# A Fourier mixer and a sentence-level expert layer on one core: the start of the pipeline and its last tile rearranged

## The chip, the cores and the metric

The kernel runs on one core of a Trainium2 chip. The time is that of the device in microseconds; the median of three runs is taken. The engines are named as in the profile: PE (TensorE, matmuls), PEld (its weight loads), DVE (VectorE), ACT (ScalarE), POOL (GpSimd) and SP (SyncE). SP and ACT start transfers on instruction rings; POOL starts those of the software queue, which can also convert fp32 to fp16 on the way.

## The reference

The input x has 8 batches of 2496 rows by 256 columns. Each batch goes through a Fourier transform over its rows, a complex mix of the columns, a soft threshold and the inverse transform, and then through one of eight experts, chosen by the mean of its rows.

```python
X = np.fft.rfft(x, axis=1)
Yr = Xr @ w_r - Xi @ w_i + b_r
Yi = Xr @ w_i + Xi @ w_r + b_i
Y = sign(Y) * np.maximum(np.abs(Y) - 0.01, 0.0)      # real and imaginary part each
y = np.fft.irfft(Y, n=2496, axis=1)
# then, per batch:
logits = y.mean(axis=1) @ w_gate                      # e = argmax, g = its softmax probability
out = g * (np.maximum(y @ w1[e], 0.0) @ w2[e])        # 256 -> 1024 -> 256
```

## The kernel before

**Stages of a batch.** The 2496 rows are seen as 39 by 64. Matmuls with a table `wa` transform over the 39 (tile `pa`), then a mix with the weights `w4` (tile `pm`), a transform over the 64 with the tables `tf` and `tm` (tile `pb`; `tm` lives in a buffer of `V2`, so the profile prints it as V), then on DVE the bias and the threshold: z, its clip `cl`, and Y as their difference. The inverse starts with table `ti` (tile `pv`, cast to `V`), goes through a scratch in DRAM (`scr`), is read back as `V2`, and ends with table `wi` (tile `pi`, cast to `ysb`). The expert layer is `ph` (first product, relu to `hs`) and `po` (second product, scaled by the gate `gbc` into `ost` and stored).

Batches 0 and 1 take a short way (`add_attn_direct`): pa with x as the stationary operand, its cast to the buffer named `XB`, and for each of ten pairs of frequencies four matmuls of 512 columns into two `pm`, two casts to `Pt`, four matmuls into `pb`, then z, clip and Y. This needs only the two plain slots of `w4`, w_r and w_i. Batches 2 to 7 (`add_attn`) need also the slots 0 and 1, which hold w_i - w_r and -(w_r + w_i); `w_products` forms them on POOL.

**Order.** All instructions of a batch are put into a list of operations with costs and dependencies, and `Schedule.run` lays them out: again and again it takes the operation that can start first by its model, and emits it on its engine. Each engine then runs its instructions in this order; the model's times set the order alone. Copies out of PSUM may go to ACT or DVE. What is emitted before the list (the first loads, the dummies) has its arrival given as constants: `X0_AT` for the parts of input 0, `W_AT` for the weights, `T_AT` for the tables, `X1_AT` for input 1. Expert work of one batch is interleaved with the transforms of the next two.

**The start.** Input 0 has eleven chunks of columns in `xin0`. Chunks 0 to 3 come as fp32 into `xf` over the rings of SP and ACT in two halves and are cast on ACT and DVE; chunks 4 to 7 and 8 to 10 come over the software queue, converted on the way, into a view of `xin0` without gaps, so that several chunks of a row form one run. Then follow on POOL the weights as fp32 (`wr`, `wm`), the tables in three parts, the biases, and input 1. Nine dummy matmuls (`WARM`) on a zeroed tile `warm` stand ahead of the first pa. The casts of the weights (`w_cast`) are operations of the list.

**The end.** The last piece of the last batch (c == 4, sp == 1) fills a bank `po` with 2 times 256 columns from 16 matmuls, one copy takes both to `ost`, and two stores on SP bring out 128 and 64 rows. In the last batch these `po` rotate through two banks.

Of the kernel before, what the change touches and what calls it, by code (L numbers as in the profile page):

```python
# [10 lines left out]
FP16 = mybir.dt.float16  # L11
# [75 lines left out]

PEN = 0.2
SLACK = 2.5


class Op:
    def __init__(self, engs, occ, lat, emit, vt, deps, allocs, dma):
        self.engs, self.occ, self.lat, self.emit = engs, occ, lat, emit
        self.vt, self.deps, self.allocs, self.dma = vt, deps, allocs, dma
        self.done = self.after = None
        self.slack = SLACK


class Tok:  # L100
# [6 lines left out]
class Schedule:  # L107
# [52 lines left out]
        return t  # L160

    def run(self):
        free = dict.fromkeys(("PE", "ACT", "DVE", "SP", "POOL"), 4.0)
        free["POOL"] = 17.0
        ring = {"SP": 7.0, "POOL": 25.0}
        todo = sorted(self.ops, key=lambda o: o.vt)
        self.log = []
        while todo:
            best = None
            seen = {e: 0 for e in free}  # L170
            for o in todo:
                if all(seen[e] > 24 for e in o.engs):
                    continue
                r = self.ready(o)
                if r is None:
                    continue
                for e in o.engs:
                    seen[e] += 1
                    s = max(r, free[e])
                    if e == "DVE" and len(o.engs) > 1:  # L180
                        s += PEN
                    k = (s, o.vt, s + o.lat[e])
                    if best is None or k < best[0]:
                        best = (k, o, e)
            (s, _, _), o, e = best
            if e == "DVE" and len(o.engs) > 1:
                s -= PEN
            todo.remove(o)
            for k in o.allocs:
                self.hist.setdefault(k.tag, []).append(k)  # L190
            free[e] = s + o.occ[e]
            o.done = s + o.lat[e]
            if o.dma:
                other = "POOL" if e == "SP" else "SP"
                t = max(ring[e], s + 1.3)
                behind = max(0.0, ring[other] - t)
                if e == "SP":
                    ext = min(2.3 * o.dma, behind)
                    ring[other] += ext / 2.3
                else:  # L200
                    ext = min(0.43 * o.dma, behind)
                    ring[other] += min(2.3 * behind, o.dma)
                ring[e] = t + o.dma + ext
                o.done = ring[e] + o.slack
            self.log.append((s, e, o))
            o.emit(e)
# [3 lines left out]
def kernel(  # L210
# [27 lines left out]
        return ctx.enter_context(tc.tile_pool(name=name, bufs=bufs, **kw))  # L238

    XROW = 2 * D + 16  # L240
    WARM = 9
    BUFS = {"XT": 2, "hs": 2, "z": 3, "V": 6}
    cpool = pool("consts", 1)
    xpool = pool("xp", 2)
# [17 lines left out]
    def load_now(b, cuts, hold=None):  # L262
# [14 lines left out]

    xin0 = xpool.tile([117, NG // 2, XROW], FP16, name="xin").rearrange(  # L280
        "p g c -> p (g c)")[:, 0 : NG * D].rearrange("p (g c) -> p g c", c=2 * D)
    xf = hpool.tile([117, 4, 2 * D], FP32, name="hs")
    xv = x[0].rearrange("(a n) c -> a n c", n=N2)
    XH = ((0, 2), (2, 4))

    def x0_part(eng, j, c0, c1, dst):
        eng.dma_start(
            out=dst[39 * j : 39 * j + 39, c0:c1],
            in_=xv[:, 21 * j + 2 * c0 : 21 * j + 2 * c1, :].rearrange(
                "a (g i) c -> a g (i c)", i=2))  # L290

    warm = cpool.tile([P, 512], FP16, name="warm")
    nc.vector.memset(warm, 0.0)
    x0_part(nc.sync, 0, 0, 2, xf)
    x0_part(nc.scalar, 1, 0, 2, xf)
    x0_part(nc.sync, 2, 0, 2, xf)
    nc.scalar.dma_start(out=wa, in_=d_wa.ap())
    x0_part(nc.sync, 0, 2, 4, xf)
    x0_part(nc.scalar, 1, 2, 4, xf)
    x0_part(nc.sync, 2, 2, 4, xf)  # L300
    for c0, c1 in ((4, 8), (8, 11)):
        for j in range(3):
            x0_part(nc.gpsimd, j, c0, c1, xin0)
    wr = opool.tile([P, 2, D], FP32, name="ost")
    wm = opool.tile([P, 2, D], FP32, name="ost")
    nc.gpsimd.dma_start(out=wr, in_=w_r.rearrange("(t p) c -> p t c", p=P))
    nc.gpsimd.dma_start(out=wm, in_=w_i.rearrange("(t p) c -> p t c", p=P))

    pw = psum.tile([P, 512], FP32, tag="o", name="po", bufs=BANKS["o"])
    for _ in range(WARM):  # L310
        nc.tensor.matmul(pw, warm[:, 0:P], warm)
    tf = cpool.tile([P, NK1, P], FP16, name="tf")
    ti = cpool.tile([P, NK1, P], FP16, name="ti")

# [12 lines left out]
                                ap=[[0, P], [1, D]]))  # L327
        nc.gpsimd.dma_start(out=ti[:, k0:k9], in_=d_ti.ap()[:, k0:k9])
    bias2 = cpool.tile([P, D], FP32, name="bias2")


    w4 = cpool.tile([P, 2, 4, D], FP16, name="w4")
    e0 = cpool.tile([P, 1], FP16, name="e0")
    nc.sync.dma_start(out=e0, in_=d_e0.ap())
    wg = cpool.tile([P, 2, E], FP32, name="wg")
    nc.sync.dma_start(out=wg, in_=moe_w_gate.rearrange("(t p) e -> p t e", p=P))
    iot = cpool.tile([P, E], FP32, name="iot")
    nc.sync.dma_start(out=iot, in_=d_iota.ap())
    wi = cpool.tile([120, 117], FP16, name="wi")
    nc.sync.dma_start(out=wi, in_=d_wi.ap())  # L340
    wg16 = cpool.tile([P, 2, E], FP16, name="wg16")
    xin1 = load_now(1, (0, NG // 2))


    X0_AT, X1_AT = (4.3, 5.6, 8.8, 10.5), 25.0
    W_AT, T_AT = 11.2, (13.0, 15.5, 18.0)

# [2 lines left out]
    gbc_t, w1s_t, w2s_t = {}, {}, {}  # L352
    COPY = {"ACT": nc.scalar.copy, "DVE": nc.vector.tensor_copy}
    DIRECT = 2
    HOLD = 9
    LATE = -0.12
    PERIOD, SPAN, SHIFT = 49.5, 1.4, 0.6
# [1 line left out]
    def bank(nm, tag):  # L359
        return psum.tile([P, 512], FP32, tag=tag, name=nm, bufs=BANKS[tag])  # L360

    def w_cast(t, src):
        def emit(eng):
            COPY[eng](out=w4[:, :, t], in_=src)  # L364
        return S.evac(460, emit, 0, deps=[S.fixed(W_AT)])

    w_in = [w_cast(2, wr), w_cast(3, wm)]

    def bias_halves(eng):
        for i in range(2):  # L370
# [1 line left out]
            COPY[eng](out=bias2[s], in_=bias[s, i])  # L372
    b_in = S.evac(400, bias_halves, 0, deps=[S.fixed(T_AT[0])])

    def w_products(_):

        nc.gpsimd.tensor_sub(out=w4[:, :, 0], in0=wm, in1=wr)
        nc.gpsimd.tensor_scalar_mul(out=wr, in0=wr, scalar1=-1.0)
        nc.gpsimd.tensor_sub(out=w4[:, :, 1], in0=wr, in1=wm)
    w_late = S.op("POOL", 4.0, w_products, 1.0, deps=list(w_in))  # L380

    def wg_cast(eng):
        COPY[eng](out=wg16, in_=wg)
    wg_in = S.evac(20, wg_cast, 0.5, deps=[S.fixed(12.0)])
    t_in = [S.fixed(T_AT[0 if k1 < 4 else 1 if k1 < 12 else 2])
            for k1 in range(NK1)]
    first_V2 = S.tok("V2", 2)
# [2 lines left out]

    def x_cast(c):
        def emit(eng):
            COPY[eng](out=xin0[:, c], in_=xf[:, c])
        return S.evac(500, emit, -30 + c, deps=[S.fixed(X0_AT[c // 2])])

    x_cast_ops = [x_cast(c) for c in range(4)]
    c1, c2 = [S.fixed(X0_AT[2])], [S.fixed(X0_AT[3])]
    xdone = {0: [x_cast_ops[:2], x_cast_ops[2:], c1, c1, c2, c2],
             1: [S.fixed(X1_AT)]}
    xin_t[0], xin_t[1] = xin0, xin1  # L400
    xtok = {b: S.tok("xin", 2) for b in range(B)}
# [5 lines left out]
    def add_load(b):  # L407
        def emit(_):

            hold = V2_t[b - 2][0:1, 20, 0:2]  # L410
            xin_t[b] = load_now(b, (0, NG // 2), hold)
        vt = (b - 2) * PERIOD
        o = S.op("POOL", 1.6, emit, vt, deps=V2op[b - 2],
                 allocs=[xtok[b]],
                 dma=7.0)
        o.after = xdone[b - 1][0] if b > 2 else w_late
        xdone[b] = [o]

    def vt_of(b):
# [479 lines left out]
    def add_moe(b, y_ops, yk, gate):  # L899
        w, gb_op, wk = gate  # L900
        v0 = b * PERIOD
        for c, (ns, nl) in enumerate(NCH):
# [32 lines left out]
            for sp in range(2):  # L935
                tago = "o" if b < B - 1 else "h"
                ok = S.tok(tago, BANKS[tago])
                oc = {}
                for q in range(4):
                    v = v0 + PERIOD * (c * 8 + 6 + 4 * sp + q) / 44  # L940

                    def mm(_, sp=sp, q=q, nl=nl, cell=cell, oc=oc, tag=tago):
                        if q == 0:
                            oc["p"] = bank("po", tag).rearrange(
                                "p (i c) -> p i c", i=2)
                        i = q // 2
                        s0 = min((2 * sp + i) * P, nl - P)
                        for ft in range(4 * (q % 2), 4 * (q % 2) + 4):
                            nc.tensor.matmul(  # L949
                                oc["p"][:, i, :],  # L950
                                cell["hs"][:, ft, s0 : s0 + P],
                                w2s_t[b][:, ft, :],
                                start=(ft == 0), stop=(ft == E - 1))
                    m = S.mm([256] * 4, mm, v,
                             deps=h_ops[: 4 + 4 * (q % 2)],
                             after=m2 if q else None,
                             allocs=[ok] if q == 0 else [])
                    m2 = m
                    hk.rel.append(m)
                    wk.rel.append(m)  # L960

                def ev(eng, oc=oc):
# [4 lines left out]
                    else:  # L967
                        nc.vector.tensor_scalar_mul(out=ost, in0=oc["p"],
                                                    scalar1=gbc_t[b])
                e = S.evac(560, ev, v, deps=[m2, gb_op])  # L970
                ok.rel.append(e)

                def st(_, ns=ns, nl=nl, sp=sp, oc=oc):
                    ost = oc["o"]
# [6 lines left out]
                    else:  # L981
# [1 line left out]
                                          in_=ost[:, 0, :])  # L983
                        nc.sync.dma_start(out=out[b, r0 + P : ns + nl, :],
                                          in_=ost[64:P, 1, :])
                S.op("SP", 0.3, st, v, deps=[e], dma=0.75)

    for b in range(B):
        if b >= 2:
# [32 lines left out]
```

## Time and profile before

| what | value |
|---|---|
| median of 3 runs | 441.6 us (441.52 to 442.1) |
| span of the profiled run | 441.3 us |
| mean granted PE clock | 0.985 |
| PE busy | 424.7 us, 96% |
| DVE, ACT, POOL busy | 288.9, 328.6, 45.2 us |
| DMA | 80.31 MB, mean 182 GB/s |
| first pm, first z, first ph of batch 0 | start at 15.37, 19.58, 57.15 us |

A busy share is an average over the span. In the views in order of time the columns are start, duration, engine, line, operation and tiles, and in brackets the idle time of the engine before it with what ended it. In the chain of waits each piece has its start, its length and what it is, followed back from the last instruction. The table of stretches gives for each interval the busy time of the engines, the granted PE clock as a share of full speed, and what the DMA moved, counted as bytes written.

### The profile page before, as it was taken

The numbers are of one execution on the slowest core, as the hardware profiler recorded it, in microseconds if no ns is written. First come the engines' busy times: TensorE is split into PE (matmuls) and PEld (weight loads), VectorE is DVE, ScalarE is ACT, GpSimd is POOL, SyncE is SP. The second block draws the span as 40 slices with busy tenths as digits, with TensorE's granted clock in tenths as the row PEclk, the third lists the DMA queues.
The fourth block names the chain that finished last, engine by engine and source line by source line (L and its number), as shares of the span: only waits on it lengthen the run. The fifth ranks groups of instructions, "written<-read, shape, count | busy, mean of one in ns | idle before, by whom it ended". The sixth has DMA issues, their size and how long they took to land.

```text
span 441.3 us, 9023 instructions
## 1 busy us (share of the span) xinstructions
PE 424.7 (96%) x3387; PEld 300.9 (68%) x3387; DVE 288.9 (65%) x605; ACT 328.6 (74%) x636; POOL 45.2 (10%) x69
## 2 busy tenths in 40 slices
PE   4888999999999999999999999999999999999996
PEld 1555566677677866778677876778667787676764
DVE  1496965298866787687966887678976877322110
ACT  2787887777967778777867778677777778678674
POOL 5920300021000200020000200020000010000000
PEclk8698999999999999999999999999999999999999
DMA  7998996899979988699988999699978456472222
GB/s 166 276 183 176 170 211 162 239 207 206 202 230 213 186 174 220 199 199 215 189 256 193 177 189 220 219 199 197 188 211 230 127 134 126 130 161 67 71 73 91
DMA packets 98961, 80.31 MB, mean 182 GB/s; under 512 B 8000, under 2 KB 91889, under 8 KB 98917
## 3 DMA queue, kind: packets, MB, share of 16 engines
q1 hardware_dynamic: 75499, 58.17, 48.9%
q0 software_dynamic: 23184, 21.22, 30.3%
q8 instruction: 26, 0.43, 0.4%
q10 hardware_dynamic: 234, 0.35, 0.3%
q14 instruction: 18, 0.15, 0.1%
HBM read 59.36 MB, written 38.80 MB: 222 GB/s over the span
## 4 chain that ended last, share of the span: by engine, by line
PE 77%; DVE 9%; DMA 7%; ACT 3%; issue 2%; SPq 1%; POOL 0%; ACTq 0%; POOLq 0%; DVEq 0%
PE po L949 28%; PE ph L917 26%; PE pm L693 8%; PE pi L788 3%; PE pa L591 3%; PE pv L436 3%; DMA xin<-in_x_dram 3%; PE px L655 3%; PE pm L514 2%; DMA V<-scr 2%; DVE z L556 2%; DMA hs<-in_x_dram 2%; DVE Y L567 1%; DVE cl L565 1%; DVE Y L735 1%
## 5 line engine op out<-in xcount | busy, mean ns | idle before, releaser
L929 ACT ACTIVATE hs<-ph 128x512 f16<-128x512 f32 (+1 forms) x296 | 170.2, 592 | 73.6 <-PE ph L917 68.4
L949 PE MATMUL po<-w2s,hs 128*128 128x256 f16 x1280 | 180.6, 272 | 0.0
L917 PE MATMUL ph<-ysb,w1s 128*128 128x512 f16 (+1 forms) x640 | 179.8, 374 | 0.5 <-ACT ysb L809 0.5
L949 PEld LDWEIGHTS <-hs 128*128 128x128 f16 x1280 | 123.3, 98 | 51.7 <-issue 2.2
L917 PEld LDWEIGHTS <-w1s 128*128 128x128 f16 x640 | 61.4, 98 | 21.5 <-issue 0.7
L965 ACT ACTIVATE ost<-po,gbc 128x512 f32<-128x512 f32 x78 | 53.7, 689 | 13.0 <-PE po L949 13.0
L735 DVE TENSOR_TENSOR Y<-z,cl 64x512 f16<-64x512 f16 x120 | 50.4, 420 | 2.8
L707 DVE TENSOR_TENSOR tt<-pm,bias 128x512 f16<-128x512 f32 x60 | 38.6, 684 | 19.4 <-PE pm L693 19.4
L693 PE MATMUL pm<-w,XT 128*128 128x256 f16 x360 | 50.0, 273 | 0.4
L693 PEld LDWEIGHTS <-XT 128*128 128x128 f16 x360 | 34.2, 98 | 12.8 <-DVE XT L674 3.8
L931 DVE TENSOR_SCALAR hs<-ph 128x512 f16<-128x512 f32 (+1 forms) x24 | 16.5, 686 | 38.5 <-PE ph L917 33.8
L716 DVE TENSOR_TENSOR z<-pm,tt 128x512 f16<-128x512 f32 x60 | 38.4, 679 | 2.9 <-PE pm L693 2.9
L444 ACT CAST V<-pv 128x512 f16<-128x512 f32 x55 | 32.5, 612 | 2.1 <-PE pv L436 1.5
L803 DVE CAST ysb<-pi 128x468 f16<-128x468 f32 (+1 forms) x41 | 23.0, 582 | 16.8 <-PE pi L788 16.5
L663 DVE CAST XT<-px 128x512 f16<-128x512 f32 x32 | 21.6, 689 | 16.5 <-PE px L655 16.3
L601 ACT CAST A<-pa 120x512 f16<-120x512 f32 x50 | 28.1, 603 | 1.3 <-PE pa L591 1.1
L436 PE MATMUL pv<-Y,ti 128*128 128x256 f16 x160 | 25.9, 272 | 2.5 <-DVE Y L567 2.1
L803 ACT CAST ysb<-pi 128x468 f16<-128x468 f32 (+1 forms) x55 | 25.8, 534 | 2.3 <-PE pi L788 2.2
L514 PE MATMUL pm<-w,XB 128*128 128x512 f16 x80 | 24.7, 428 | 1.9 <-ACT w L364 1.0
L525 ACT CAST Pt<-pm 128x512 f16<-128x512 f32 x35 | 19.9, 589 | 6.7 <-PE pm L514 6.7
L788 PEld LDWEIGHTS <-V 120*128 120x128 f16 x352 | 21.0, 98 | 4.0 <-issue 0.7
L788 PE MATMUL pi<-wi,V 120*128 120x117 f16 x352 | 23.2, 214 | 0.3
(70 smaller groups left out, 332.8 us busy)
## 6 DMA issues: line engine op xcount, KB each, us to landing
out_dram<-ost SPq DMA_DIRECT2D x72, 256.0 KB
scr<-V SPq DMA_DIRECT2D x80, 128.0 KB
V<-scr SPq DMA_DIRECT2D x24, 420.0 KB
xin<-in_x_dram POOLq DMA_DIRECT2D x21, 429.0 KB, 9.3
XB<-fwd SPq DMA_DIRECT2D x30, 256.0 KB
fwd<-A SPq DMA_DIRECT2D x18, 360.0 KB
w1s<-in_moe_w_dram POOLq DMA_DIRECT2D x8, 512.0 KB, 8.3
w2s<-in_moe_w_dram POOLq DMA_DIRECT2D x8, 512.0 KB, 7.8
```

The source lines that it names most:

```text
L436: nc.tensor.matmul(pv[:, D * i : D * i + D], ti[:, k0 + i, :], cell["Y"](i))
L514: nc.tensor.matmul(pm, A_t[b]["A"][:, ch, k1, :, :], w4[:, ch, 2:4, :].rearrange("p t c -> p (t c)"), start=(ch == 0), stop=(ch == 1))
L693: nc.tensor.matmul(pm[:, D * a : D * a + D], cell["X"][:, ch, a, t].rearrange("p i k -> p (i k)"), w4[:, ch, t, :], start=(ch == 0), stop= ...
L707: nc.vector.tensor_add(out=cell["tt"][:, r], in0=cell["T", 2].rearrange("p (a c) -> p a c", a=2), in1=bias[:, r].unsqueeze(1).to_broadcast ...
L716: nc.vector.tensor_add(out=cell["z"][:, r], in0=cell["T", 1 - r].rearrange("p (a c) -> p a c", a=2), in1=cell["tt"][:, r])
L735: nc.vector.tensor_sub(out=Y[64 * r : 64 * r + 64, :, i], in0=cell["z"][s, r], in1=cell["cl"][s, r])
L788: nc.tensor.matmul(pi[:, 117 * i : 117 * i + M], V2[:, g, ch * P : ch * P + P], w)
L803: COPY[eng](out=yv[:, :, 12 * gb : 12 * gb + 3 * nf].rearrange("p a (g j) -> p a g j", j=3), in_=pi[:, 0 : 117 * nf].rearrange("p (g a j) ...
L917: nc.tensor.matmul(ph[:, 0:nl], w1s_t[b][:, ch, fc * P : fc * P + P], ysb_t[b][:, ch, ns : ns + nl], start=(ch == 0), stop=(ch == 1))
L929: nc.scalar.activation(out=o, in_=i, func=AFT.Relu)
L949: nc.tensor.matmul(oc["p"][:, i, :], cell["hs"][:, ft, s0 : s0 + P], w2s_t[b][:, ft, :], start=(ft == 0), stop=(ft == E - 1))
L965: nc.scalar.activation(out=ost, in_=oc["p"], func=AFT.Copy, scale=gbc_t[b])
```

## The change

The change has six parts.

1. Chunks 0 and 1 alone (`XF = 2`) come over the rings as fp32; chunks 2 to 6 and 7 to 10 come over the software queue. `xin0` now has rows with gaps (`XROW`), so that each run read is one chunk of a row, 2 KB. It is meant to let the ring's packets through sooner.
2. w_r and w_i are converted by the software queue straight into slots 2 and 3 of `w4`; the casts go.
3. The slots 0 and 1 are formed later, on DVE, from a second fp32 load of the weights over SP into a buffer of `ysb` (`w_loads`, `w_products`, due at 52 in the model's time). POOL has no arithmetic left.
4. Dummies are operations of the list that `run` may place wherever PE would wait until 12.6 in the model's time, to hold PE's clock up until the mix. A copy of one element of `warm` on ACT draws its table load to the start.
5. The bias copies, the weight casts' places and the small loads are operations or constants with new times; the constants for arrivals change.
6. The last piece of the last batch uses two banks: its first 128 rows are scaled on DVE and stored by SP, its last 64 rows are scaled on ACT and stored over ACT's own queue.

```diff
-    x0_part(nc.sync, 0, 0, 2, xf)
-    x0_part(nc.scalar, 1, 0, 2, xf)
-    x0_part(nc.sync, 2, 0, 2, xf)
+    x0_part(nc.sync, 0, 0, XF, xf)
+    x0_part(nc.scalar, 1, 0, XF, xf)
+    x0_part(nc.sync, 2, 0, XF, xf)
     nc.scalar.dma_start(out=wa, in_=d_wa.ap())
-    x0_part(nc.sync, 0, 2, 4, xf)
-    x0_part(nc.scalar, 1, 2, 4, xf)
-    x0_part(nc.sync, 2, 2, 4, xf)
-    for c0, c1 in ((4, 8), (8, 11)):
+    nc.scalar.copy(out=warm[0:1, 0:1], in_=warm[0:1, 1:2])
+    for c0, c1 in X0_CUTS:                               # (2, 7), (7, 11)
         for j in range(3):
             x0_part(nc.gpsimd, j, c0, c1, xin0)
-    nc.gpsimd.dma_start(out=wr, in_=w_r.rearrange("(t p) c -> p t c", p=P))
-    nc.gpsimd.dma_start(out=wm, in_=w_i.rearrange("(t p) c -> p t c", p=P))
+    nc.gpsimd.dma_start(out=w4[:, :, 2], in_=w_r.rearrange("(t p) c -> p t c", p=P))
+    nc.gpsimd.dma_start(out=w4[:, :, 3], in_=w_i.rearrange("(t p) c -> p t c", p=P))
-    for _ in range(WARM):
-        nc.tensor.matmul(pw, warm[:, 0:P], warm)
...
-    w_in = [w_cast(2, wr), w_cast(3, wm)]
+    w_in = [S.fixed(W_AT)]
+    def w_loads(_):
+        for i, w in enumerate((w_r, w_i)):
+            nc.sync.dma_start(out=wf[:, i], in_=w.rearrange("(t p) c -> p t c", p=P))
     def w_products(_):
-        nc.gpsimd.tensor_sub(out=w4[:, :, 0], in0=wm, in1=wr)
-        nc.gpsimd.tensor_scalar_mul(out=wr, in0=wr, scalar1=-1.0)
-        nc.gpsimd.tensor_sub(out=w4[:, :, 1], in0=wr, in1=wm)
-    w_late = S.op("POOL", 4.0, w_products, 1.0, deps=list(w_in))
+        nc.vector.tensor_sub(out=w4[:, :, 0], in0=wf[:, 1], in1=wf[:, 0])
+        nc.vector.scalar_tensor_tensor(out=w4[:, :, 1], in0=wf[:, 0], scalar=-1.0,
+                                       in1=wf[:, 1], op0=ALU.mult, op1=ALU.subtract)
+    o = S.op("SP", 0.8, w_loads, W_LATE, deps=[S.fixed(W_LATE)], dma=1.5)
+    w_late = S.op("DVE", 1.4, w_products, W_LATE, deps=[o])
...
+    for i in range(WARM):                                # WARM = 60, COLD = 10
+        def dummy(_):
+            nc.tensor.matmul(pw, warm[:, 0:P], warm)
+        o = S.op("PE", 0.43 if i < COLD else 0.216, dummy, 1e6 + i)
+        o.until = WARM_END                               # 12.6
...
-                        if q == 0:
-                            oc["p"] = bank("po", tag).rearrange(
-                                "p (i c) -> p i c", i=2)
+                        if q == 0 or q == 2 and last:
+                            oc["p"] = oc["p", q // 2] = bank(
+                                "po", tag).rearrange("p (i c) -> p i c", i=2)
...
+                if last:
+                    e = S.op("DVE", 0.45, ev_first, v, deps=[m1, gb_op])
+                    ok.rel.append(e)
+                    e = S.op("ACT", 0.45, ev_last, v, deps=[m2, e])
+                    ok2.rel.append(e)
```

## The prediction

> **What bounds the kernel now.** I read the engine shares first, then the 40 slices, then the chain of waits, then the start and the tail in order of time. TensorE (PE) is busy for 96% of the span, and all slices but the first few stand at 9:
>
> ```profile
> PE 424.7 (96%) x3387; PEld 300.9 (68%) x3387; DVE 288.9 (65%) x605; ACT 328.6 (74%) x636; POOL 45.2 (10%) x69
> PE   4888999999999999999999999999999999999996
> PEclk8698999999999999999999999999999999999999
> ```
>
> After the first stage the kernel is bound by its matmuls; over 180 to 230 us the table of stretches shows PE busy 50.00 of 50.00 us. Time can be won only before PE fills up (about 57 us), at the end, or where the granted clock is below full. The chain of waits names the start:
>
> ```profile
> 1.88 8.19 DMA hs<-in_x_dram
> 10.10 0.44 DVE xin L393
> 10.58 2.33 PE pa L478 x20
> 12.93 1.88 ACT XB L489 x5
> 14.81 0.52 ACT w L364
> 15.37 3.59 PE pm L514 x8
> 18.98 0.59 ACT Pt L525
> 19.58 0.70 DVE z L556
> ```
>
> The second fp32 half of input 0 lands at 10.07 us. Then come the column transforms (pa), their casts, the cast of the mix weights, eight mix matmuls (pm) and, at 19.58, the first z on VectorE (DVE). From there to 37.60 nearly all pieces of the chain are DVE (z, clip, Y for ten pairs), so an earlier first z moves the whole rest. Eight pm in 3.57 us are 0.43 us each; between 19.31 and 33 two take 0.43 us. In the stretches of one us the clock is 1.00 at 7 to 8, 0.50 from 9 to 19, and 1.00 again from 19. Two DVE rows are also longer than their like, beside the weight sums on GpSimd (POOL):
>
> ```profile
> 20.71 0.80 DVE L567 TENSOR_TENSOR Y<-z,cl 128x512 f16<-128x512 f16 x1
> 22.36 1.26 DVE L565 TENSOR_SCALAR cl<-z 128x512 f16<-128x512 f16 x1
> 23.66 0.42 DVE L567 TENSOR_TENSOR Y<-z,cl 128x512 f16<-128x512 f16 x1
> 20.61 1.51 POOL L378 TENSOR_SCALAR ost<-ost 128x512 f32<-128x512 f32 x1
> 22.21 1.26 POOL L379 TENSOR_TENSOR w<-ost 128x512 f16<-128x512 f32 x1
> ```
>
> The clip at 22.36 ends just after POOL does at 23.47. And the tail:
>
> ```profile
> 433.88 3.27 PE L949 MATMUL po<-w2s,hs 128*128 128x256 f16 x28
> 435.93 0.69 ACT L965 ACTIVATE ost<-po,gbc 128x512 f32<-128x512 f32 x1 [1.30 <-PE po L949]
> 437.24 0.69 ACT L965 ACTIVATE ost<-po,gbc 128x512 f32<-128x512 f32 x1 [0.63 <-PE po L949]
> 437.95 0.35 SPq L982 DMA_DIRECT2D out_dram<-ost  x1
> 438.35 0.47 SPq L984 DMA_DIRECT2D out_dram<-ost  x1
> ```
>
> From the end of the last issue (438.82) to 441.3 are 2.48 us of landing.
>
> **What the Trainium skill says.** "TensorE: Matmul & The Clock Gate", Part 1: PE runs at half rate by default and is released after a busy window of about 3.4 us; the window is free-running, so where it falls differs from run to run. The trace agrees: nine dummies from 1.31 to 5.33 run at 0.43 us, pa at 7.62 runs warm, and clock changes near 8.75, 18.98, 39.46 and 42.87 are 3, 6 and 1 times 3.41 us apart. "SBUF — State Buffer", "Who interferes with whom": VectorE in a two-port mode and GpSimd lock each other out for a whole instruction; the clip above agrees. "ScalarE: Activation LUTs", "What ACT_TABLE_LOAD costs": 1283 ns; the trace has 1.28 us at 5.65. "DMA: Bandwidth & Descriptors", "Queues, rings and completion order": each DMA engine serves its queues in turn, a packet at a time. This fits the second half landing 4.4 us after the first, beside GpSimd transfers in larger runs.
>
> **The change part by part.**
>
> *Input.* Two chunks of eleven on the instruction rings instead of four, and runs of 2 KB read on the software queue. The first half landed at 5.65; I take 5.3 for xf, since the rings now meet smaller packets. The total read stays: 2.56 MB of x, then 0.52 MB of weights. The DMA engines are full from 4 us on (share 0.91 to 1.14), and traffic with a cast moves 155 to 171 GB/s written at 20 to 22 us, that is 310 to 340 read, where uncast tables move 337 to 344: it is the read that is paid. So the end of x hardly moves. POOL's waits before its later issues end at 8.64, 10.68, 12.16 as the six x transfers land; the last landed by 13.2 us. I take 10 us for chunks 2 to 6, 12.5 for 7 to 10 (11.5 to 13.2).
>
> *Weights cast by the ring.* They landed at 13.5 and 14.3 (issues 4.61 and 5.36, plus 8.9), and will again, as the bytes read are the same. What goes is the 0.52 us of ACT cast on the chain, and the DVE cast beside it.
>
> *Dummies.* In the built order PE has 13 dummies, 8 pa, 8 dummies, 16 pa, 6 dummies, 20 pa, 3 dummies, then the mix. The first dummy now waits for ScalarE, because the small copy that draws the table load forward writes into `warm`: issues to 1.85, load 1.28, copy about 0.2, so they begin at 3.45, not 1.31. What stands behind them on PE is every real matmul. A window that is wholly busy ends between 6.9 and 10.3. Warm at 6.9: 8 dummies at 0.427 and 5 at 0.216 end at 7.95; 8 pa at 0.054 (0.43 us of weight loads at 7.61), 8 dummies, 16 pa, 6 dummies end at 12.3. Warm at 10.3: that point is 14.0. I take 13.2. Then 20 pa; ScalarE has three 480-column casts behind the first pair, 0.56 each, so the mix starts 2.1 later: 14.4 to 16.1, I take 15.3, against 15.37. The table load itself is worth nothing on the path: pa waited for the second half anyway.
>
> *Warm mix.* Eight pm take 1.73 instead of 3.57. DVE waits in order for both bias halves (the second landed at 16.50), then casts the fourth pm (0.69, from 1.9 after the start of the mix), then adds the first z. First z = 15.3 + 1.9 + 0.7 = 17.9 (17.4 at best, by the bias; 18.7 at worst). Gain 19.58 - 17.9 = 1.7.
>
> *Products to DVE.* POOL no longer works from 19.21 to 23.47. The two long rows shrink by 0.80 - 0.42 and 1.26 - 0.30, together 1.3 us on the DVE chain. ScalarE could take some of it back: per pair it has three casts of 0.53 to 0.59 and is busy 8.90 of 10 us from 30 to 40. But its casts start earlier too, and it loses 1.46 us of weight and bias copies. I take 1.3 (0.6 to 1.3). The products on DVE (two rows of about 0.6) are emitted behind casts of A, near 71 us, where DVE is busy 5.44 of 10: hidden. The second fp32 load of the weights, 0.52 MB at some 315 GB/s, is 1.7 us of DMA near 50 us; behind it on the SyncE queue stand writes of V. The load of input 2, beside it, lands by about 65 and is used at 69.24: hidden.
>
> *Tail.* The last tile's second half gets its own PSUM bank from two, so its 8 matmuls wait until ScalarE has read the tile before (435.93 + 0.69 = 436.62) where they would start at 436.1: +0.57. The last cast has 256 columns: halfway between the 0.30 of the 8-column exponent row and the 0.69 of 512 columns is about 0.49 (-0.2), and the store is issued from ScalarE's own queue at once (0.32 to 0.65) instead of second on SyncE (0.87 from 437.95): about -0.5. Sum -0.15 (-0.4 to +0.2).
>
> Sum: 1.7 + 1.3 + 0.15 = 3.15. From PE's 1210th row on the built order is the same, so the gain carries through. 441.6 - 3.15 = 438.4.
>
> **The rivals.**
> 1. *The clock also stays up in the second gap.* PE stands idle around 36.9 to 39.38 and the next eight pm again take 3.53; with another phase of the window they take 1.73: 438.4 - 1.8 = 436.6. For it: the phase is chance. Against: the gap is the same.
> 2. *The shift is eaten downstream.* Input 1 is issued at 16.82 to 18.4 behind the same tables and landed 9.9 to 12.2 later, so as late as 30.6; its pa began at 33.74, so only 3.1 us are free. With 1.7 us of reload showing as well, and a late HAM window, 3.15 - 1.7 = 1.45 remains: 440.2. Against: PE waits for DMA once, 0.3 us, in 30 to 130 us.
> 3. *The dummies hold up the data.* If the clock isn't released, 30 dummies at 0.427 and 44 pa at 0.105 end at 3.45 + 17.4 = 20.9; DVE's z follows at 20.9 + 2.6 = 23.5, 3.9 later than before; less 1.45: 444.1, slower. Against: 4 us of dummies did release it before.
>
> **How the numbers follow.** Chances: forecast 0.55, rival 1 0.22, rival 2 0.15, rival 3 0.08. The range reaches from rival 1's 436.6 to 440.6, which takes in rival 2 and the worst z (18.7, stall gain 0.6, tail +0.2: 441.6 - 0.9 - 0.6 + 0.2 = 440.3); rival 3 and the lucky half of rival 1 are left out. Faster (below 440.7): 0.84; rival 2 lies half on each side of that bound; within 0.2%: 0.09; slower: 0.07, which is rival 3.
>
> **What would show it.** Right: dummies from about 3.4; pa and pm at full clock; mix near 15.3 and z near 17.9; clip and Y at 0.3 and 0.42 from the start; a PE wait of about 0.6 for ScalarE before the last eight matmuls; the same rows from 60 us on, some 3 us earlier. Wrong: a clock of 0.50 over the first mix, a z before 17 or after 19, PE waiting for input 1 or 2, or a DVE wait on the reloaded weights.

## The result, and the profile after

The changed kernel takes 444.9 us (444.04 to 446.07), the kernel before 441.6 beside it: 1.0076 times, 95% interval 1.0048 to 1.0104. It is slower by 3.3 us, where 3.2 us less was forecast. Here and below, the few executions that lie more than 1.5% above the fastest of the same kernel are left out of the medians.

The start is faster than forecast. In order of time (start, duration, engine, line, operation, tiles, in brackets the idle time ahead and what ended it):

```profile
3.45 1.89 PE L392 MATMUL po<-warm 128*128 128x512 f16 x4 [3.45 <-ACT warm L302]
14.20 1.89 PE L528 MATMUL pm<-w,XB 128*128 128x512 f16 x8
16.85 0.69 DVE L570 TENSOR_TENSOR z<-pb,bias 128x512 f16<-128x512 f32 x1
```

The dummies begin at 3.45, the mix at 14.20 (15.37 before), its eight matmuls take 1.89 us, and the first z comes 2.7 us earlier. The first expert matmul comes at 52.23 instead of 57.15. All of that is lost by 121 us. The page's busy shares hardly tell it; its slices do, and so does the table of what PE waited for (total, times, longest), after and, in the last line, before:

```profile
PE 425.5 (96%) x3408; PEld 301.0 (68%) x3408; DVE 288.9 (65%) x609; ACT 327.5 (74%) x632; POOL 41.5 (9%) x66
PEclk9999998999999999999999999999999999999999
```
```profile
PE pa L605 <- DMA xin<-in_x_dram: 5.2, 2, 3.7
PE pa L492 <- DMA xin<-in_x_dram: 1.9, 1, 1.9
```
```profile
PE pa L591 <- DMA xin<-in_x_dram: 0.3, 1, 0.3
```

The low slice of PEclk has moved from the first 45 us to the seventh slice, 67 to 78 us. Before, that 0.3 us, for input 3 at 109 us, is the only wait for a load of batch 1 or later. Now there are three: 1.9 us for input 1, 3.7 for input 2, 1.5 for input 3. The chain of waits (start, length, piece) runs through them:

```profile
17.78 13.76 DMA xin<-in_x_dram
31.68 0.58 PE pa L492 x8
...
36.73 1.90 PE pm L528 x8
...
50.73 17.45 DMA xin<-in_x_dram
68.31 1.93 PE pa L605 x5
...
98.43 13.47 DMA xin<-in_x_dram
```

The first five pa of batch 2 in PE's row, before and after:

```profile
69.08 1.24 PE L591 MATMUL pa<-xin,wa 117*120 117x512 f16 x5
```
```profile
68.31 1.93 PE L605 MATMUL pa<-xin,wa 117*120 117x512 f16 x5 [3.73 <-DMA xin<-in_x_dram]
```

They take 1.24 us at full clock, and 1.93 after. The table of stretches around them (busy time of PE, PEld, DVE, ACT, POOL with instruction counts, then clock, DMA share, GB/s) says why:

```profile
64.00:66.00 2.00, 0.58 (x4) 0.08 (x1) 0.00 (x0) 0.94 (x2) 0.00 (x0) 1.00 0.62 137
66.00:68.00 2.00, 0.00 (x0) 0.00 (x0) 0.00 (x0) 0.00 (x0) 0.00 (x0) 1.00 0.21 65
68.00:70.00 2.00, 1.69 (x5) 0.91 (x6) 0.84 (x2) 1.00 (x2) 0.00 (x0) 0.69 0.01 3
70.00:72.00 2.00, 2.00 (x8) 1.34 (x7) 1.41 (x3) 1.10 (x3) 0.00 (x0) 0.50 0.46 83
```

PE sits idle from 64.58 to 68.31, and then, with work there again, the clock is at half until 72.2. "TensorE: Matmul & The Clock Gate", Part 1, of the Trainium skill puts the fall after an idle window of about 3.4 us; this wait of 3.73 agrees, though shorter waits were enough in two other runs (last section). At the 41st ph the kernel is 1.5 us behind the kernel before (80.22 against 78.75), and at the 101st, after the wait for input 3, 2.6 behind (120.54 against 117.95); to the last ph that hardly changes (436.49 against 433.70).

The loads of input 2, from issue to landing over its three parts, in the list of its tile, before:

```profile
DMA to landing us min/median/max: 10.9/13.0/14.7
```

and after:

```profile
DMA to landing us min/median/max: 10.7/14.2/17.4
```

PE needs all three, so the maximum counts: landed at 67.11 before, where PE came at 69.08, and at 68.17 after, where PE came at 64.58. The tail:

```profile
439.46 1.03 PE L966 MATMUL po<-w2s,hs 128*128 128x256 f16 x8 [0.39 <-ACT ost L983]
```

The last eight matmuls wait 0.39 us for ScalarE, and PE ends 4.00 us after the start of the last ph instead of 3.45. From PE's end to the span's end are 3.92 instead of 4.16.

The profiled executions aren't the median ones: that of the kernel before took 442.96 us, that of the changed kernel 446.07. Their difference, 3.1 us, is close to that of the medians.

### The profile page after: what moved, and what is told of

It reads as the page before. It is cut to its first block, busy times and chain, and to the rows that moved or that the text cites. A ratio compares the mean times of both kernels' runs of the same rounds, so it can differ in the third digit from the quotient of the medians.

```text
span 444.4 us, 9069 instructions
## 1 busy us (share of the span) xinstructions
PE 425.5 (96%) x3408; PEld 301.0 (68%) x3408; DVE 288.9 (65%) x609; ACT 327.5 (74%) x632; POOL 41.5 (9%) x66
## 4 chain that ended last, share of the span: by engine, by line
PE 72%; DMA 14%; DVE 6%; POOL 3%; issue 2%; ACT 1%; SPq 1%; POOLq 0%; ACTq 0%
PE po L966 28%; PE ph L931 24%; DMA xin<-in_x_dram 12%; PE pm L707 7%; PE pa L605 3%; PE pi L802 3%; PE pv L450 3%; PE px L669 2%; DMA V<-scr 2%; DVE Y L749 2%; POOL xin L276 1%; DVE z L730 1%; PE pm L528 1%; DVE tt L721 1%; DVE XT L677 1%
## 5 line engine op out<-in xcount | busy, mean ns | idle before, releaser
L721 DVE TENSOR_TENSOR tt<-pm,bias 128x512 f16<-128x512 f32 x60 | 38.6, 684 | 19.7 <-PE pm L707 19.6
L677 DVE CAST XT<-px 128x512 f16<-128x512 f32 x34 | 23.0, 689 | 19.4 <-PE px L669 19.2
L458 ACT CAST V<-pv 128x512 f16<-128x512 f32 x57 | 33.4, 608 | 1.5 <-PE pv L450 1.1
L615 ACT CAST A<-pa 120x512 f16<-120x512 f32 x52 | 29.1, 600 | 6.2 <-PE pa L605 6.0
L605 PE MATMUL pa<-xin,wa 117*120 117x512 f16 x66 | 22.9, 403 | 5.2 <-DMA xin<-in_x_dram 5.2
```

The costliest lines, as they stand in the source:

```text
L605: nc.tensor.matmul(pa[0:120, :], wa, xin_t[b][:, gp, 0 : 2 * D])
L721: nc.vector.tensor_add(out=cell["tt"][:, r], in0=cell["T", 2].rearrange("p (a c) -> p a c", a=2), in1=bias[:, r].unsqueeze(1).to_broadcast ...
```

## The experiments

Names say what a kernel is: `nr` is the changed kernel without the second load of the weights, `before` the kernel before. Times are medians, with the 95% interval of the ratio to the kernel before, run beside it on the same chip. Runs of different experiments can be on different chips, where the kernel before has medians of 441.6 to 442.2, so differences under 1 us between experiments say little.

**1. Is it the reload?** `no_reload` takes it away; the products are formed on VectorE from the fp16 weights that are there. `before_plus_load` adds the two loads to the kernel before, into a buffer that nobody reads.

```diff
-        for i, w in enumerate((w_r, w_i)):
-            nc.sync.dma_start(out=wf[:, i], in_=w.rearrange("(t p) c -> p t c", p=P))
+        pass
...
-        nc.vector.tensor_sub(out=w4[:, :, 0], in0=wf[:, 1], in1=wf[:, 0])
+        nc.vector.tensor_sub(out=w4[:, :, 0], in0=w4[:, :, 3], in1=w4[:, :, 2])
...
```

> The changed kernel without the second load of the mix weights: the two product slots of w4 are formed on VectorE from the fp16 slots, at the same place; the order on every engine is otherwise the same. Theory R (the 0.52 MB reload on SyncE's ring slows the load of input 2 beside it): the last part of input 2 lands at 63.5 to 64.5 us (8.7 us after the expert weights at 55.1, as before the change), PE waits under 0.5 us for it, the clock stays up, and the time is 437.5 to 439. Rival O (the earlier start alone brings PE too early to input 2, whose place in the queue is fixed by the expert weights ahead of it): it lands at 66.5 or later, PE waits 2 us or more, time 442.5 to 444.5.

> The kernel before with the same 0.52 MB fp32 load added on SyncE's queue behind the sixth store of V of batch 1, as in the changed kernel; its data isn't used. R: input 2's last part lands near 71 instead of 67.1, PE (which comes to it at 69.1) waits about 2 us and may lose its clock for 3.4 us; 443.5 to 445.5. O: no wait, 441.3 to 442.

Measured: no_reload 440.1 us (0.9938 to 0.9979), before_plus_load 443.5 (1.0027 to 1.0063). The chain of no_reload:

```profile
50.58 14.47 DMA xin<-in_x_dram
...
65.18 1.26 PE pa L602 x5
```

The last part of input 2 lands 3.0 us sooner after its issue than with the reload, PE waits 1.2 us for it instead of 3.7, and the five pa take 1.26: the clock stays. So 0.52 MB on another queue are worth 4.8 us to the changed kernel (444.9 against 440.1). That fits the Trainium skill, "DMA: Bandwidth & Descriptors", "Queues, rings and completion order": the DMA engines serve their queues in turn, so that the reload gets its share though it was issued later. But theory R had the sign and not the size: it expected a landing by 64.5 and 439 us at most, where input 2 lands at 65.05 and 1.2 us of wait remain. And before_plus_load's profiled execution has input 2 only 0.8 us later after its issue (15.56 against 14.71) and no wait over 0.5 us for it or a later input, so the reload isn't the whole story. That execution, 442.29 us, was among the three fastest of 14; what the slower ones do is in no trace.

**2. Is it the tail?**

```diff
-                last = b == B - 1 and c == 4 and sp == 1
+                last = False
```

> The changed kernel with the last tile's end as before (one bank, one copy of 512 columns on ScalarE, two stores on SyncE). If the second bank's wait and the store on ScalarE's queue cost what the two traces differ by after the last ph (PE end 3.35 later, span 3.11 later, ph 2.79 later), the time falls by 0.3 (0.1 to 0.5), to about 444.5. If the new tail saves the 0.15 of the forecast, it rises to 445.0. Input 2 is waited for as before, 3.7 us.

> Both edits together. R: 437.2 to 438.8, faster than the kernel before by 0.6% or more, and the difference to the run without the reload is that of the tail alone (0.3 lower). O: 442 to 444.5.

Measured: old_tail 444.1 (1.0006 to 1.006), from 440.6 to 446.6; no_reload_old_tail 440.6 (0.9951 to 0.9993) against no_reload's 440.1. Once the old tail is 0.8 us below, once 0.5 above, so the tail makes no difference that can be measured. old_tail's times lie in two groups, 440.6 to 441.6 (six of 18) and 443.4 to 446.6. Its profiled execution, of the second group, has a wait of 2.7 us for input 2 and the low clock after it; the six fast ones have a mean granted clock of 0.998 to 1.000, eleven of the twelve others 0.996 or less. So a good part of the loss comes and goes from one execution to the next. The changed kernel itself ran four times, at 444.0 to 446.1.

**3. Load input 2 sooner.** DMA stands nearly idle from 38 to 40 us (share 0.07). `in2_gap` issues input 2 right behind batch 0's expert weights and drops the small copy that held it until batch 0's gathers (V<-scr) had landed. The order on the other engines is unchanged here and in experiment 4.

```diff
+            if b == 2:
+                return
...
             w1s_t[b], w2s_t[b] = w1s, w2s
+            if b == 0:
+                xin_t[2] = load_now(2, (0, NG // 2))
```

> The changed kernel with one thing moved: input 2's three loads are put on the GpSimd queue right behind the expert weights of batch 0 (about 24.5 us instead of 49.2) and without the copy that held them back; the orders of PE, ACT, DVE and SP stay as they are, and the weight reload stays. Theory L (the loss is the late landing of input 2 and what follows from it: the wait, the lower clock after it, input 3's chain): input 2 lands before 50, PE no longer waits at batch 2's first forward matmul, and the time is 437.5 to 439.5, below the kernel before. Rival O (the matmul order or the reload itself costs the time elsewhere, so that the wait only moves): above 441.5. A third, G (the load now delays batch 0's expert weights, 37.97 before, past the first expert matmul at 52.2, or the stores and gathers of the inverse stage): a new wait on w1s, V2 or scr, 440 or more.

> The same move of input 2, on the kernel without the reload (products formed from the fp16 weights already there). L: the 1.2 us wait that was left without the reload goes too, 437.5 to 439, and equal to in2_gap within 0.5 us, since a reload that delays no awaited load costs nothing. O: within 0.5 us of 440.1, as without the reload alone. If the reload costs by itself (SP ring, DVE operands), in2_gap is over 1 us above this run.

Measured: in2_gap 444.8 (1.0036 to 1.0096) and nr_in2_gap 444.0 (1.0021 to 1.006): the expectation fell, and rival G came true. Input 2 lands at 45.73, but the gathers, issued 2 us later, land at 54.20 instead of 48.66. PE's row, from in2_gap in order of time:

```profile
47.73 0.59 PE L804 MATMUL pi<-wi,V 120*128 120x117 f16 x8 [1.77 <-DMA V<-scr]
52.33 0.95 PE L804 MATMUL pi<-wi,V 120*128 120x117 f16 x15 [1.38 <-DMA V<-scr]
54.25 0.28 PE L804 MATMUL pi<-wi,V 120*128 120x39 f16 x3 [0.98 <-DMA V<-scr]
```

The hold protected the gathers. Two variants on this base, nine dummies and the products back on GpSimd, were run beside them:

> nr_in2_gap with 9 dummies in place of 30: the PE clock falls back before the first mix, whose eight matmuls take 3.6 us again instead of 1.9. L (what the start gains goes through to the end once input 2 waits for nothing): 1.2 to 2.2 us above nr_in2_gap. Rival H (the start's gain is hidden by input 1, which PE waits for at 30 anyway): within 0.5 us of nr_in2_gap.

> nr_in2_gap with the two weight products formed on GpSimd beside the first mix again, as in the kernel before: first z to ninth z 14.7 us instead of 13.2. L: 0.8 to 1.6 us above nr_in2_gap, if the start goes through. H: within 0.5 us, since PE then waits that much less for input 1 at 30 to 31.7.

Measured: nr_gap_nine 444.8 and nr_gap_pool 443.9, within 0.8 and 0.1 us of nr_in2_gap. On a base that waits for gathers this says little of either part; experiment 5 asks again.

**4. Keep the hold, exchange two loads.** The expert weights of batch 1 are needed at 105 us, yet go ahead of input 2, needed at 64. `in2_ahead` exchanges them, reload and all else as in the changed kernel.

```diff
         def wl(_):
+            if b == 1:
+                late_w.append(wl_now)
+            else:
+                wl_now()
+        def wl_now():
...
             xin_t[b] = load_now(b, (0, NG // 2), hold)
+            if b == 2:
+                late_w.pop()()
```

> The changed kernel with two loads exchanged on the GpSimd queue: input 2 keeps its hold on batch 0's gathers, but goes ahead of the expert weights of batch 1 (needed only at about 105 us) instead of behind them. All else, the reload too, stays, and so do the orders of the other engines. Theory L, as it stands now (from 41 to 65 us the DMA carries more than it can, and the loss is that input 2 comes last there): the gathers land 1 to 3 us earlier than 48.66, input 2 lands by 60, no wait at batch 2's first forward matmul and none for V2 at 39 to 60, 437.5 to 439.5. Rival O (matmul order, or the reload by itself): 441.5 or more. Rival S (the weights of batch 1 now come late): a wait on w1s near 105.

> The same exchange without the reload. L: no wait for input 2, 437.3 to 439, that is 1 to 2.5 us below the 440.1 without the reload alone, and within 0.7 us of in2_ahead, as a reload that delays no awaited load is free. O: within 0.5 us of 440.1.

> The kernel before with the same exchange of input 2 and batch 1's expert weights. L: its PE waits 0.3 us for input 2, so there is nothing to win: within 0.6 us of before. Rival B (the exchange relieves the gathers of batch 0 or the clock's second gap too): 1 us or more below before, and then part of what in2_ahead wins is no repair of the change.

Measured: in2_ahead 439.8 (0.9933 to 0.9975), nr_in2_ahead 438.9 (0.9916 to 0.9959; four runs), before_in2_ahead 441.5 (0.9963 to 1.0009). From in2_ahead, input 2's landing and PE's row:

```profile
DMA to landing us min/median/max: 6.4/9.4/12.9
```
```profile
64.33 1.24 PE L607 MATMUL pa<-xin,wa 117*120 117x512 f16 x5
```

Input 2 lands at 63.65, 0.7 us ahead of PE; no wait, and the clock is 1.00 from 60 to 74. The weights, with 19.3 us to landing (w2s), are there at 71.5. This exchange turns the changed kernel from 3.3 us slower than the kernel before to about 2 us faster. On the kernel before it does nothing, as there PE came after the landing; the wait of 0.3 us that its expectation names is for input 3. The reload, with no awaited load to delay, no longer shows beyond the scatter. Two points of the expectation were wrong: input 2 lands at 63.65, not by 60, and the gathers at 48.60, not earlier, so what batch 1's weights delayed was input 2 alone.

**5. Where is the rest of the start's gain?** PE still waits 1.9 us for input 1 in in2_ahead. `ahead_no_dummies` sets WARM = 0, `nr_ahead_nine` WARM = 9; `nr_ahead_pool` forms the products on GpSimd again at the start; `ahead_w0_held` holds batch 0's expert weights by a small copy until input 1 has landed.

```diff
-    WARM, COLD, WARM_END = 60, 10, 12.6
+    WARM, COLD, WARM_END = 0, 10, 12.6
```
```diff
-        nc.vector.tensor_sub(out=w4[:, :, 0], in0=w4[:, :, 3], in1=w4[:, :, 2])
+        nc.gpsimd.tensor_sub(out=w4[:, :, 0], in0=w4[:, :, 3], in1=w4[:, :, 2])
...
-    w_late = S.op("DVE", 1.4, w_products, W_LATE, deps=[o])
+    w_late = S.op("POOL", 4.0, w_products, 1.0, deps=list(w_in))
```
```diff
+            if b == 0:
+                nc.gpsimd.tensor_copy(out=w1s[96:97, 0, 0:2],
+                                      in_=xin_t[1][96:97, 0, 0:2])
```

> nr_in2_ahead with 9 dummies: first mix at the lower clock again, first z 1 to 2 us later. L (with input 2 in time, the start's gain goes through): 1.0 to 2.0 us above nr_in2_ahead. Rival H (the wait for input 1 near 31 takes the start's gain): within 0.5 us.

> in2_ahead with no dummy at all. The first mix runs at the lower clock: its eight matmuls take 3.5 us instead of 1.9, and batch 0's first matmuls before it are slower too. Theory T (the start goes through): 1.5 to 3 us above in2_ahead. Rival H (the wait for input 1 takes it): first z 2 to 3 us later, but batch 1's first forward matmul within 0.5 us of 31.7, and the time within 0.7 us of in2_ahead.

> nr_in2_ahead with the products formed on GpSimd beside the first mix, as before. First z to ninth z about 14.5 us instead of 13.2 on T and on H. T: 0.8 to 1.6 us above nr_in2_ahead's 438.9. H: within 0.5 us of it, since PE then waits less for input 1.

> in2_ahead, and batch 0's expert weights (needed at 52 us) are held by a two-element copy until input 1's last third has landed, so that they no longer share the DMA with it. Theory I (input 1 is late because 2 MB of expert weights run beside it, and PE's 1.9 us wait for it passes to the end): input 1 lands 1.5 to 3.5 us earlier, no wait for it, 437.3 to 438.8. Rival P (input 1's own packets or the tables ahead of it set its landing): landing within 0.7 us of 31.6, same time as in2_ahead, 439.8. Rival G (the weights then run into batch 0's gathers): gathers later than 50.5, a wait of PE on them, slower than in2_ahead.

Measured: nr_ahead_nine 439.6 (0.9942 to 0.9974), ahead_no_dummies 439.9 (0.9943 to 0.9977), nr_ahead_pool 441.5 (0.9973 to 1.0004), ahead_w0_held 442.8 (0.9986 to 1.0035).

*Dummies.* ahead_no_dummies' first mix is slow, its z is 2.1 us later than in2_ahead's, and yet its time is the same:

```profile
14.73 3.57 PE L530 MATMUL pm<-w,XB 128*128 128x512 f16 x8 [0.33 <-PE pa L494]
...
31.79 0.59 PE L494 MATMUL pa<-wa,xin 117*128 117x120 f16 x8
```

The same row in in2_ahead:

```profile
31.71 0.58 PE L494 MATMUL pa<-wa,xin 117*128 117x120 f16 x8 [1.87 <-DMA xin<-in_x_dram]
```

Both start batch 1 at the same time: one comes late (input 1 had landed at 30.19), the other waits for input 1, which landed at 31.58. What the warm first mix gains is hidden there, and 439.9 against 439.8 shows none of it. In nr_ahead_nine the clock fell to 0.50 at 11 to 13 us too, but came back ahead of the mix, so that run tells less.

*Products.* Back on GpSimd they cost 2.6 us (441.5 against 438.9; 1.9 against the repeat in experiment 6), more than either theory had. First z to tenth z takes 17.9 us where nr_in2_ahead takes 15.8, and then the clock of batch 1's mix falls. Stretches of nr_ahead_pool:

```profile
35.00:38.00 3.00, 1.56 (x22) 1.16 (x20) 2.86 (x6) 2.80 (x8) 0.00 (x0) 1.00 0.79 207
38.00:41.00 3.00, 2.98 (x8) 1.14 (x9) 0.00 (x0) 1.48 (x4) 0.00 (x0) 0.50 0.15 46
```

and of in2_ahead:

```profile
35.00:38.00 3.00, 2.08 (x16) 1.23 (x17) 1.59 (x3) 2.44 (x8) 0.00 (x0) 1.00 0.62 149
38.00:41.00 3.00, 2.82 (x18) 1.46 (x15) 1.75 (x4) 1.78 (x5) 0.00 (x0) 1.00 0.05 13
```

With the products on GpSimd the late z starve PE at 35 to 38, and the eight matmuls behind run at half clock. This isn't so in every execution: of the five profiled kernels with the products on GpSimd at the start, the clock fell at batch 1's mix in three (before, before_in2_ahead, nr_ahead_pool) and stayed in two (before_plus_load, nr_gap_pool); of the fourteen with them late on VectorE it fell there in none. Nor is the clock what the 2.6 us are: seven of nr_ahead_pool's 13 runs have a mean granted clock of 1.000, where one fall (3.4 us at half, of 440) costs 0.004, and their median is 441.5 too. That leaves the late z.

*Input 1.* Holding the expert weights brought it 0.5 us earlier (31.10), as rival P has it, while the gathers came to 50.86 (rival G) and input 2 to 67.21: PE waits 2.4 us for it again, and loses its clock.

**6. Is the move of the products all there is?** `before_ahead_dve` is before_in2_ahead with the products late on VectorE from fp16; the load of input 2, which was held behind them on GpSimd, no longer is. nr_in2_ahead is repeated beside it.

```diff
-    w_late = S.op("POOL", 4.0, w_products, 1.0, deps=list(w_in))
+    w_late = S.op("DVE", 1.4, w_products, 52.0, deps=[S.fixed(52.0)] + w_in)
...
-        o.after = xdone[b - 1][0] if b > 2 else w_late
+        o.after = xdone[b - 1][0] if b > 2 else None
```

> The kernel before with input 2 ahead of batch 1's expert weights (which alone made no difference, 441.46) and the two products formed on VectorE from the fp16 weights, late, in place of GpSimd beside the first mix; loads of input 0, weight casts, dummies and tail as before. Theory Q (the products are the gain, by the evictions that they slowed and by the clock of batch 1's mix): first z at 19.6 as before, ninth z by 33.5, clock of batch 1's mix 1.00, and 439 to 440, no more than 1 us above nr_in2_ahead. Rival E (the earlier start has its share too): 440.2 to 441.2, halfway between 441.5 and 438.9.

> nr_in2_ahead again: 438.9 as before on L, with more runs; 439.8 or more if the first four were lucky, and then equal to in2_ahead.

Measured: before_ahead_dve 440.3 (0.9932 to 0.9969) and nr_in2_ahead_2 439.6 (0.9914 to 0.9968). The edit takes 1.2 us off before_in2_ahead's 441.5. That is just above Q's 439 to 440 and inside E's 440.2 to 441.2. Whether the earlier start adds to it can't be said: over both sets of runs nr_in2_ahead has a median of 439.3 in 19 runs, 1.0 us less, but the intervals overlap. So between Q and E it stays open. The profiled execution doesn't decide it, as its clock happened to rise at 14.72, ahead of the first mix (first z at 17.8, where 19.6 was expected); batch 1's mix was at 1.00, as Q has it.

## Why the prediction was wrong

*The step that failed* is one sentence on the reload: "The load of input 2, beside it, lands by about 65 and is used at 69.24: hidden." It has three faults, which together brought PE to a load that hadn't landed.

1. The landing. 65 is what an issue near 52 and the median of 13.0 us give; PE needs the last part, which landed at 67.11. The slack was 2.0 us, not 4.
2. The use. 69.24 is where the kernel before uses it. The prediction's own gain of 3.15 us moves that to about 66, ahead of 67.11 even with no reload; in no_reload PE did wait, 1.2 us, for a landing at 65.05. In the trace after, PE came at 64.58.
3. The price. The reload was costed as 1.7 us of DMA near 50 us and then at nothing, being hidden. It made the last part of input 2 land 3.0 us later after its issue (17.45 against 14.47), and the low clock and input 3 came on top. From the profiles of in2_ahead and after: 4.0 us at batch 2's first pa (64.33 and 68.31), 1.7 more by the 41st ph (clock), 1.5 more by the 101st (input 3), together 7.2, about what the spans differ by (437.3 and 444.4). By the medians the late load cost 5.1 us (444.9 and 439.8), as these two executions lie on opposite sides of theirs.

"So the gain carries through" thus failed as well: the order on PE is the same, but the loads' landing is no part of that order.

*A second step failed, by less:* the 1.7 us for the warm mix. in2_ahead, with input 2 in time, is 1.9 us faster than the kernel before, not 3.15. The gain put on the mix was an amount of slack, not of time: in the trace of in2_ahead PE waits 1.87 us for input 1, and experiment 5 finds the same time without a single dummy.

*Rival 2* came nearest, with input 1 and the reload, but it named neither the wait for input 2 nor the clock, and its size was off: it let 1.7 us of the gain go, where forecast and result lie 6.5 us apart. The argument against it, that PE waits for DMA once, 0.3 us, was read the wrong way round: a wait of 0.3 us for input 3 means that this load had no slack at all. *Rival 3* has a figure close to the result, 444.1, by luck: what it needs, a first mix at the lower clock, didn't come.

*Right:* the dummies begin at 3.45; pa and pm run at full clock; the contention on VectorE was worth 1.3 us, and first to ninth z took 13.19 instead of 14.59 us (1.40). The casts by the ring brought no wait. The products on VectorE, at 71.80, brought no wait, and the 0.57 us on the last PE rows measured 0.55; the tail is about zero, not -0.15, within its range.

*Start too late in the forecast:* mix at 14.20 and z at 16.85, both ahead of the ranges given. The clock was released at 7.3 us, near the early end of the 6.9 to 10.3 allowed; the mix came 1.75 us after the start of the last 20 pa, where 2.1 was taken; and the bias, which was to hold z until 17.4, was being copied at 14.62.

*Rival 1* came true as well: the clock stayed up in the second gap, and less by chance than the rival had it: that went with the place of the products (experiment 5). It was lost again with the rest.

*Open:* why the last part of a load lands 3 to 4 us behind the others while DMA's share is only 0.2 (66 to 68 us) was not tried, nor whether input 1 can be issued earlier, ahead of tables. That the late z alone make up what the products cost on GpSimd is argued, not shown.

## What to carry to other kernels

When a change makes an early stage faster, list each load that the engine meets later and set the landing of its last part against the new time of use, not the old one; a short wait, or none by 2 us, is slack that the gain itself uses up. Before adding traffic, ask which awaited load is in flight then, and put what is needed first ahead in its queue: here two loads exchanged were worth 5 us. A gain at the start counts only up to the next wait that doesn't move with it.

## What the hardware showed that was not expected

- 0.52 MB over SyncE's ring were issued at 53.8 and 54.3 us while input 2 was in flight. Their second half landed 10.3 us after its issue, and input 2's last part 3.0 us later than without them, counted from its issue, more than the 1.7 us of DMA time reckoned for it. In the kernel before the same pair cost that part 0.8 us.
- One load in three parts lands one part after another, 10.7, 14.2 and 17.4 us after their issues; while PE waits for the last, DMA's share is 0.21 (66 to 68 us).
- A wait of a few microseconds at PE can be paid twice: in the trace after 3.73 us idle, then 3.4 us at half clock, which do 1.7 us less work. Idle time shorter than the 3.4 us of the page named above was enough in old_tail and ahead_w0_held, and the measurement decides:

```profile
67.22 1.36 PE L605 MATMUL pa<-xin,wa 117*120 117x512 f16 x5 [2.71 <-DMA xin<-in_x_dram]
```
```profile
67.34 2.36 PE L607 MATMUL pa<-xin,wa 117*120 117x512 f16 x5 [2.44 <-DMA xin<-in_x_dram]
```

Their clocks stood at 0.50 from 69 to 71 us and from 67 to 70. In the last 3.41 us ahead of the falls PE had been busy for 0.44 (after), 1.03 and 1.35 us. no_reload_old_tail waited 2.66 us for input 1 and kept its clock, so the length of the wait alone doesn't decide; the times in two groups (old_tail, 440.6 to 441.6 and 443.4 to 446.6) fit that.
